# First batch of an attention and mixing kernel: more places for queries, later weight loads, a wider first mixing product, and another order of the opening

## The chip, the cores and the metric

The kernel runs on one core of one Trainium2 chip. The metric is the device time of one execution in microseconds (us). Engines are named as the profile names them: PE is TensorE, PEld its weight loads, DVE VectorE, ACT ScalarE, POOL GpSimd, SP SyncE; SPq is SP's issuing of DMAs.

## The reference

Attention over 4 batches, 8 heads, 768 tokens of width 64: each token sees a band of 16 neighbours on either side and 24 block summaries (maximum of the keys, mean of the values of each 32 tokens). Its output goes through a token mixing of rank 32 and a two-layer channel network of width 2048. Weights `U`, `V`, `w_ch1`, `w_ch2` come as 64-bit floats, all results are float32.

```python
k_sum = k.reshape(B, H, nb, block, D).max(axis=3)
v_sum = v.reshape(B, H, nb, block, D).mean(axis=3)
scores_all = np.concatenate([scores_l_masked, scores_s + np.log(block)], axis=-1)
a = softmax(scores_all)                          # 120 keys per 64 queries after packing
x = (a @ np.concatenate([v, v_sum])).reshape(B, S, 512)
u = x + (x.transpose(0, 2, 1) @ U @ V).transpose(0, 2, 1)
out = u + np.maximum(u @ w_ch1, 0.0) @ w_ch2
```

## The kernel before

Batches are done one after the other, each overlapping the next. Batch 0 has nothing to hide behind: its attention and mixing run in an opening of some 51 us, whose order is written by hand as a string of words, `START`. A loop takes the words one by one and records each word's instructions on the engines concerned; every engine then runs its own instructions strictly in that order, and SP issues the loads in that order. After the opening comes batch 0's channel network, 16 stretches `f`, each with a piece of up product and down product, with batch 1's attention spread between them.

The words, `h` a head, `i = 2h + a` a half of it:

- `lk h`, `lq h`, `lv p`, `lm`, `li`, `lu`, `lr`, `la f`, `lb f`: loads of keys, queries (two DMAs of 96 KB), values of two heads (two DMAs), mask, identity, `U` and `V` as raw 64-bit words, the matrix `rep`, one weight tile of `w_ch1` (`la`) or `w_ch2` (`lb`), 512 KB each.
- `K h`: two maxima over the keys on DVE (L316). `Kd h` / `Kp h`: their four copies into the key tile (L333), on DVE or POOL.
- `S h`: 12 score products on PE (L374). `E i`: three DVE instructions with the mask and the row maximum (L400, each with a read of its sum) and three exponentials on ACT (L410). `T i`: three transposes on PE (L460), `C i` their copy on ACT (L466). `V i`: six products with the values on PE (L476). `N h`: the division by the sum on DVE (L502 to L504), which writes `x`.
- `M g`: block means of the values of four heads on PE (L292), `Mo g` their copy on ACT (L304); `Bp`, `Dp`, `Bd`, `Dd`, `Ba` `h`: their 24-row copies into the value tiles (L337), on POOL (p), DVE (d) or ACT (a). `F` prepares the matrix for `M` on DVE.
- `X`, `Xt0` to `Xt2`, `Xs`, `Xl`: `U` and `V` from 64-bit words to float32 (ACT, POOL, DVE, DVE) and their split.
- `Z k`: scaling of weight step `k`'s raw words on ACT (L142); step 0 is tile (0,0), step k is tiles (0,k) and (1,k-1). `Y k.0`, `Y k.1`, `Y k.2`: the three steps from raw words to float32 (signs L155 on POOL or L157 on DVE, then L161 and L164 on DVE). `W k`: the split in a rounded high part (ACT, L179) and a low part (L180).
- `I c`, `Io c`, `J c`, `Jo c`: mixing's first and second product and their copies for channels c, c+1; `Q`, `Qo`: spreading of `V`. `G hf.c`, `Go hf.c`: three transposes and one product on PE (L699, L707) that make the mixed rows, and their split on ACT and DVE (L719, L720). `U 0.0`: the first up product (L927), which ends the opening.

Buffers that matter here: weight tiles have five places in a ring for each of the two matrices, `weight_place(i, f)`, reused with `f % 5`. While the ring is empty, other data are put there: `raw_uv`, the target of `lu`, is `weight_place(0, 2)`, the place of the tile that `la2` loads. Queries of batch 0 have four places, `qd0`, so that `lq4` to `lq7` wait on SP until `S0` to `S3` have read theirs. PSUM's eight banks go round. In the channel network, `traffic(f, i)` loads the tiles that come later.

## Time and profile before

| | |
|---|---|
| time, median of 3 runs (lowest to highest) | 648.07 us (647.09 to 650.53) |
| profiled execution: time, and its span | 648.17 us, 646.4 us |
| PE busy of the span | 627.1 us (97%) |
| DVE, ACT, POOL busy | 361.7, 354.6, 363.3 us |
| DMA | 115.39 MB, mean 179 GB/s |

Busy times are of the span; the time that runs give is 1.8 us above the span, for what lies outside the first and last instruction. "PE acc L949 x8" is eight matmul records that write tile `acc` from line 949; a float32 product with float32 operands makes two records, so `S` shows as 24, `V` as 12, `T` as 3, `M` as 96.

### The profile page before, as it was taken

The page shows a single profiled execution, that of the slowest core. Times are in us where ns is not written, and L with a number is a line of the kernel's source. Part 1 is how long each engine was busy: PE and PEld are TensorE (multiplying, and loading weights), DVE is VectorE, ACT ScalarE, POOL GpSimd, SP SyncE. Part 2 cuts the span into 40 slices and gives each one's busy share as a digit, 9 for nine tenths or more (in the row PEclk, how much of TensorE's full clock was granted, in tenths as well). Part 3 has the DMA queues.
Part 4 walks back from the last instruction along what each step waited for, and adds up shares of the span by engine and source line. Part 5 has one row for each costly group of instructions (what it writes and reads, how often), then busy time and mean ns, then how long its engine had stood idle before and what let it go on. Part 6 is the DMA issues. An engine that isn't in the chain of part 4 may idle for free.

```text
span 646.4 us, 14559 instructions
## 1 busy us (share of the span) xinstructions
PE 627.1 (97%) x5528; PEld 563.4 (87%) x5528; DVE 361.7 (56%) x1002; ACT 354.6 (55%) x788; POOL 363.3 (56%) x391
## 2 busy tenths in 40 slices
PE   5879999999999999999999999999999999999997
PEld 4669988888888899998888899998888899998886
DVE  5779767675857596566444645565544522242223
ACT  4756766656663657675453457775453455553321
POOL 3525977965766875862246765771344565653320
PEclk9999999999999999999999999999999999999999
DMA  9897588866675169896628367887431164342002
GB/s 236 223 380 222 160 296 267 229 201 189 214 232 176 46 213 290 243 265 174 180 78 218 113 204 222 258 258 203 144 116 58 60 183 142 115 131 66 32 1 99
DMA packets 68678, 115.39 MB, mean 179 GB/s; under 512 B 6912, under 2 KB 43648, under 8 KB 68608
## 3 DMA queue, kind: packets, MB, share of 16 engines
q1 hardware_dynamic: 68608, 114.45, 58.9%
q8 instruction: 44, 0.72, 0.5%
q14 instruction: 26, 0.21, 0.1%
HBM read 90.31 MB, written 24.12 MB: 177 GB/s over the span
## 4 chain that ended last, share of the span: by engine, by line
PE 87%; DMA 4%; DVE 3%; SPq 2%; ACT 2%; issue 1%; DVEq 0%; ACTq 0%
PE acc L1316 30%; PE ps_h L1215 27%; PE acc L949 10%; PE ps_h L927 9%; PE ps_x L490 3%; PE ps_s L374 2%; PE ps_s L351 2%; DMA place<-in_w 1%; PE ps_t L460 1%; SPq L215 1%; DMA kt<-in_k 1%; PE ps_u L699 1%; DMA place<-in_v 1%; DMA place<-in_q 1%; PE ps_m L665 1%
## 5 line engine op out<-in xcount | busy, mean ns | idle before, releaser
L180 POOL TENSOR_TENSOR parts<-whole,parts 128x512 fp32r<-128x512 f32 (+1 forms) x144 | 182.3, 1273 | 162.9 <-ACT parts L179 153.1
L1316 PE MATMUL acc<-gh,parts 128*128 128x256 f32 (+1 forms) x768 | 198.2, 340 | 0.0
L1215 PE MATMUL ps_h<-op,parts 128*128 128x384 f32 x1008 | 181.7, 337 | 0.1
L1215 PEld LDWEIGHTS ps_h<-op,parts 128*128 128x128 f32 x1008 | 174.3, 188 | 2.7 <-issue 1.1
L1316 PEld LDWEIGHTS acc<-gh,parts 128*128 128x128 f32 x768 | 132.9, 189 | 17.4 <-issue 1.7
L1316 PE MATMUL acc<-gl,parts 128*128 128x256 f32 (+1 forms) x384 | 129.8, 338 | 0.2
L1288 DVE SCALAR_TENSOR_TENSOR gl<-place,gh 128x768 fp32r<-128x768 f32 x48 | 55.3, 1151 | 71.3 <-ACT gh L1284 71.2
L179 ACT CAST parts<-whole 128x512 fp32r<-128x512 f32 (+1 forms) x144 | 83.3, 583 | 3.3 <-DMA whole<-up 1.0
L1316 PEld LDWEIGHTS acc<-gl,parts 128*128 128x128 f32 x384 | 72.8, 189 | 7.5 <-DVE gl L1288 0.8
L410 ACT ACTIVATE e<-e,neg 128x120 f32<-128x120 f32 x144 | 46.5, 386 | 51.4 <-DVE neg L400 46.9
L927 PE MATMUL ps_h<-place 128*128 128x384 f32 x384 | 74.3, 342 | 0.0
L1284 ACT ACTIVATE gh<-place 128x768 fp32r<-128x768 f32 x48 | 40.5, 844 | 57.1 <-PE acc L1316 48.5
L927 PEld LDWEIGHTS ps_h<-place 128*128 128x128 f32 x384 | 66.2, 188 | 1.4 <-issue 0.4
L949 PE MATMUL acc<-place,gh 128*128 128x512 f32 x192 | 67.3, 405 | 0.0
L155 POOL TENSOR_SCALAR val<-place 128x512 f32<-128x512 f32 (+1 forms) x30 | 47.7, 1607 | 25.9 <-ACT place L142 21.4
L180 POOL TENSOR_TENSOR place<-val,place 128x512 fp32r<-128x512 f32 x29 | 38.7, 1357 | 18.3 <-ACT place L179 18.3
L742 POOL TENSOR_TENSOR op<-tmp,op 128x384 fp32r<-128x384 f32 x24 | 26.3, 1108 | 32.9 <-ACT op L738 30.2
L949 PEld LDWEIGHTS acc<-place,gh 128*128 128x128 f32 x192 | 35.9, 188 | 7.6 <-POOL place L180 0.6
L400 DVE CUSTOM_DVE_ANT_0 e<-ps_s,mask_sb 128x120 f32<-128x120 f32 x144 | 32.8, 277 | 11.3 <-PE ps_s L351 5.9
L949 PE MATMUL acc<-place,gl 128*128 128x512 f32 x96 | 37.7, 393 | 0.1
L161 DVE SCALAR_TENSOR_TENSOR val<-place,val 128x512 int32<-128x512 int32 (+1 forms) x33 | 31.7, 965 | 3.3 <-POOL val L155 3.2
L1241 DVE TENSOR_TENSOR place<-place,ps_h 128x384 f32<-128x384 f32 x24 | 13.2, 551 | 36.2 <-PE ps_h L1215 36.2
(113 smaller groups left out, 796.5 us busy)
## 6 DMA issues: line engine op xcount, KB each, us to landing
place<-in_w SPq DMA_DIRECT2D x32, 512.0 KB, 5.6
whole<-up SPq DMA_DIRECT2D x24, 512.0 KB, 4.4
whole<-down SPq DMA_DIRECT2D x24, 512.0 KB, 4.3
whole<-up SPq DMA_DIRECT2D x24, 384.0 KB, 3.4
vt<-in_v SPq DMA_DIRECT2D x48, 146.2 KB, 3.8
kt<-in_k SPq DMA_DIRECT2D x24, 288.0 KB, 5.9
there<-squares SPq DMA_DIRECT2D x16, 384.0 KB, 4.3
at<-there SPq DMA_DIRECT2D x64, 96.0 KB, 3.5
```

The lines of the kernel that those rows point to most:

```text
L155: nc.gpsimd.tensor_scalar(f32(bits), f32(hi), 0.0, None, ALU.mult)
L161: lambda lo, hi, bits: nc.vector.scalar_tensor_tensor(bits, lo, 29, bits, ALU.logical_shift_right, ALU.bitwise_or),
L179: nc.scalar.copy(hi, val)
L180: engine.tensor_tensor(lo, val, f32(hi), ALU.subtract)
L400: nc.vector.tensor_tensor_reduce(out=e[:, u, :], in0=ps[:, i * KC : (i + 1) * KC], in1=mask_sb[:, m, :], scale=-SCALE, scalar=BIG, op0=ALU ...
L410: nc.scalar.activation(e[:, u, :], e[:, u, :], AF.Exp, bias=st.neg[h][:, u : u + 1], scale=-1.0,)
L927: nc.tensor.matmul(ps[:, :NH], w_split[0, f][:, c % 2, part_w, c // 2], ut[:, c, :], start=(n == 0), stop=(n == 3 * NC - 1),)
L949: nc.tensor.matmul(acc[t], gt[:, sl], w_split[1, f][:, part_w], start=(first and j == 0), stop=(last and j == 2),)
L1215: nc.tensor.matmul(ps, a[:, sa, i], b[:, sb, i], start=(first and n == 0), stop=(n == 5), skip_group_check=not first,)
L1284: nc.scalar.activation(gh, h, AF.Relu)
L1288: nc.vector.scalar_tensor_tensor(gl, h, 0.0, f32(gh), ALU.max, ALU.subtract)
L1316: nc.tensor.matmul(place, w[:, part_w, c * P : (c + 1) * P], gt[:, q0:q1], start=(f == 0 and i == 0 and j == 0), stop=(f == NF - 1 and j = ...
```

## The change

Four things, all in batch 0's opening. Queries get eight places: three in a spare tile and five in the weight places (1,2), (1,4) and (0,4). Weight tiles (0,4), (1,3) and (1,4) are no longer loaded in the opening but by `traffic` in the first stretches; their words are gone from `START`, and the loads that follow in the opening are `la0`, `la2`, `la1`, `lb0`, `lb2`, `lb1`, `la3`. Mixing's first product for two channels is six matmuls of 256 columns instead of twelve of 128. And all words stand in another order, in which step 1's signs (`Y1.0`) are made on POOL instead of DVE, and step 0's low part (`Wp0`) too.

```diff
 START = """
-    lm lk0 lq0 lk3 lu li lq3 X K0 Kd0 S0 K3 Kd3 E1 lk2 Xt0 lk1 S3 E0 K2 lq2 E7 Kp2 lq1 S2 E6 T6 E4
...
+    lk0 lk1 lq0 lm lq1 K0 Kd0 K1 Kd1 lk3 S0 lq3 S1 lk2 E0 E3 K3 E1 K2 lv0 E2 lq2 Kp3 S3 li lv1 E6
...
-    qd0 = [t[:, j * NH : (j + 1) * NH] for j in range(3)] + [weight_place(1, 2)[:, :NH]]
+    spare = [weight_place(1, 2), weight_place(1, 4), weight_place(0, 4)]
+    qd0 = [t[:, j * NH : (j + 1) * NH] for j in range(3)]
+    qd0 += [spare[i][:, j * NH : (j + 1) * NH] for i, j in ((0, 0), (1, 0), (1, 1), (2, 0), (0, 1))]
...
-        st.qt[h] = qd0[h % 4] if st.b == 0 else qz[h % 2].rearrange("p u q -> p (u q)")[:, :NH]
+        st.qt[h] = qd0[h] if st.b == 0 else qz[h % 2].rearrange("p u q -> p (u q)")[:, :NH]
...
+    def mix_t_wide(st, c):
+
+        ps = bank("ps_m")
+        for s in range(NU):
+            g = s % 4
+            nc.tensor.matmul(
+                ps[R * g : R * g + R, : 2 * P],
+                u_sb[:, s, :],
+                st.x[:, s, c * P : (c + 2) * P],
+                start=(s < 4),
+                stop=(s + 4 >= NU),
+                tile_position=(0, R * g),
+            )
+        st.ps_m[c] = ps
...
-            split(hi, lo, val, nc.vector if k < 2 else nc.gpsimd)
+            split(hi, lo, val, engine)
...
-    turns = {k: turn_weights(k) for k in range(2)}
+    turns = {k: turn_weights(k, k in (1,)) for k in range(2)}
...
-        "I": lambda c: mix_t(st, c, 2),
+        "I": lambda c: mix_t_wide(st, c),
...
-        "W": split_weights,
+        "W": lambda k: split_weights(k, nc.vector),
+        "Wp": split_weights,
...
-            if 0 < f and f + RING - 1 < NF:
+            if f + RING - 1 < NF:
                 load_weight(0, f + RING - 1)
...
-            if 1 < f and f + RING - 2 < NF:
+            if f + RING - 2 < NF:
                 load_weight(1, f + RING - 2)
```

The opening on PE, before and then after: `place` stands for the key and query tiles, `ps_s` for a bank of scores, `ps_t` for one of transposes, `ps_n` for the block means.

```order
L374 MATMUL ps_s<-place 64x120 x36
L460 MATMUL ps_t<-ident_sb,gl 120x128 x3
L460 MATMUL ps_t<-ident_sb,gh 120x128 x9
L374 MATMUL ps_s<-place 64x120 x12
L460 MATMUL ps_t<-ident_sb,gh 120x128 x3
L292 MATMUL ps_n<-place,means_w 32x65 x48
```

```order
L376 MATMUL ps_s<-place 64x120 x48
L462 MATMUL ps_t<-ident_sb,gl 120x128 x9
L462 MATMUL ps_t<-ident_sb,gh 120x128 x6
L294 MATMUL ps_n<-place,means_w 32x65 x48
L462 MATMUL ps_t<-ident_sb,gh 120x128 x6
L462 MATMUL ps_t<-ident_sb,gl 120x128 x3
```

Four heads' scores now stand ahead of the first transpose, where there were three.

The loads on SP around the first weight tiles, before and then after. `place` with `in_v` is a pair's values, with `in_w` a weight tile; in square brackets stand the semaphores that SP waits for ahead of the issue, `DMAHW` those of earlier DMAs and the others those of engines.

```order
L236 DMA place<-in_v 96x780 [waits DMAHW1_49]
L236 DMA place<-in_v 96x780 [waits DMAHW2_49]
L792 DMA place<-in_w 128x1024 [waits DMAHW3_49]
L792 DMA place<-in_w 128x1024 [waits DMAHW4_49]
L792 DMA place<-in_w 128x1024 [waits DMAHW5_49]
L1049 DMA rep_sb<-in_rep 128x128 [waits DMAHW6_49]
```

```order
L238 DMA place<-in_v 96x780 [waits DMAHW1_49]
L238 DMA place<-in_v 96x780 [waits DMAHW2_49]
L809 DMA place<-in_w 128x1024 [waits DMAHW3_49]
L809 DMA place<-in_w 128x1024 [waits DMAHW4_49,DMAHW6_49,DVE_49,Pool_49]
L1066 DMA rep_sb<-in_rep 128x128 [waits DMAHW5_49]
L809 DMA place<-in_w 128x1024
```

The second weight tile is now `la2`, which waits for the readers of `raw_uv` on POOL and DVE; it was the last one. Behind it on SP now stand `lr`, `lb0`, `la1` and the rest.

ACT at the end of the mixing, before and then after: `L142` / `L144` scales a weight tile (`Z1`), `t_st` is what `Jo` writes, `vm_st` what `Qo` writes, `t_862` and `t_855` what `Io` writes.

```order
L142 ACTIVATE place<-place 128x512 [waits DMAHW5_49]
L142 ACTIVATE place<-place 128x512 [waits DMAHW7_49]
L691 CAST t_st<-ps_r 128x256 [waits PE_49]
L1039 CAST vm_st<-ps_v 128x384 [waits PE_49]
L678 COPY t_862<-ps_m 128x256 [waits PE_49]
```

```order
L144 ACTIVATE place<-place 128x512 [waits DMAHW7_49]
L144 ACTIVATE place<-place 128x512 [waits DMAHW6_49]
L708 CAST t_st<-ps_r 128x256 [waits PE_49]
L181 CAST place<-val 128x2x256 [waits DVE_49]
L1056 CAST vm_st<-ps_v 128x384 [waits PE_49]
L695 COPY t_855<-ps_m 128x256 [waits PE_49]
```

`Z1` stands ahead of the same copies as before, and step 0's split has moved in between.

## The prediction

> **What bounds the kernel now.** I read the two windows on either side of the first up product first. Columns: length, then busy time and records of PE, PEld, DVE, ACT and POOL, granted clock, DMA share, GB/s.

> ```profile
> 0.00:51.10 51.10, 37.06 (x741) 30.43 (x742) 35.07 (x173) 30.51 (x86) 19.05 (x47) 1.00 0.95 281
> 51.10:646.40 595.30, 590.00 (x4789) 533.02 (x4788) 326.68 (x831) 324.12 (x703) 344.24 (x344) 1.00 0.56 170
> ```

> After 51.1 us PE is busy 590.0 of 595.3 us, and the change takes nothing from it there. In the opening PE is idle 14.0 us, with no other engine full and the DMA engines at 95%. So the change is worth what it does to the start of the first up product, 51.10; I look for that time alone. The timeline of PE gives pace and waits (start, length, what, idle before and its releaser):

> ```profile
> 5.37 1.99 PE L374 MATMUL ps_s<-place 64*64 64x120 f32 x24 [5.37 <-DVE place L333]
> ...
> 13.48 0.89 PE L460 MATMUL ps_t<-ident_sb,gl 128*120 128x128 f32 x3
> 14.17 2.13 PE L460 MATMUL ps_t<-ident_sb,gh 128*120 128x128 f32 x9
> ...
> 17.72 1.60 PE L292 MATMUL ps_n<-place,means_w 96*32 96x65 f32 x96
> ...
> 22.89 0.85 PE L374 MATMUL ps_s<-place 64*64 64x120 f32 x24
> ...
> 26.29 0.45 PE L476 MATMUL ps_x<-place 120*64 120x65 f32 x8 [0.54 <-issue]
> ...
> 35.20 1.19 PE L292 MATMUL ps_n<-place,means_w 120*32 120x65 f32 x68 [1.23 <-issue]
> ...
> 41.40 2.44 PE L476 MATMUL ps_x<-place 120*64 120x65 f32 x76 [2.10 <-issue]
> ...
> 48.06 0.49 PE L699 MATMUL ps_u<-ident_sb,x 128*128 128x128 f32 x3
> ...
> 48.56 0.49 PE L699 MATMUL ps_u<-ident_sb,x 128*128 128x128 f32 x3
> ...
> 51.10 4.51 PE L927 MATMUL ps_h<-place 128*128 128x384 f32 x24
> ```

> Two things stand in it. The same 24 score records take 1.99 us early and 0.85 later, three transposes 0.69 us early (13.48 to 14.17): PE starts at half pace, though the granted clock is 1.00. And three waits end by "issue", in the midst of equal matmuls, where no semaphore is due. Counted in the trace's PE records, these places are 256 instructions apart (a matmul record and its weight load are two). One DMA of the instruction queue falls before each:

> ```profile
> q8 instruction: 44, 0.72, 0.5%
> ```

> 0.72 MB in 44 is 16 KB, 256 instructions of 64 bytes. So PE gets its program in blocks of 256, and a block seems to be asked for when the one before is begun: 26.29 to 35.20 is 8.9 us, 35.20 to 41.40 is 6.2, both with the DMA engines full. PE's matmuls of such a block take 3 to 5 us in the opening, 22 later, so only the opening can wait for it.

> [...]

> Now SP and the loads: the longest of SP's waits (total, times, longest), its first weight tiles, and windows as above.

> ```profile
> SPq L215 <- PE ps_s L374: 4.6, 1, 4.6
> ```

> ```profile
> 27.55 1.38 SPq L792 DMA_DIRECT2D place<-in_w x3
> ```

> ```profile
> 2.20:18.00 15.80, 10.38 (x131) 7.98 (x135) 9.58 (x64) 7.23 (x23) 4.81 (x12) 1.00 1.02 269
> ...
> 18.00:20.00 2.00, 2.00 (x99) 1.91 (x88) 1.72 (x10) 2.00 (x9) 0.72 (x3) 1.00 0.62 178
> 20.00:22.00 2.00, 1.29 (x29) 0.97 (x26) 1.87 (x7) 2.00 (x7) 1.78 (x5) 1.00 0.45 109
> ...
> 36.00:40.00 4.00, 3.30 (x87) 2.80 (x76) 3.09 (x5) 3.48 (x10) 2.91 (x5) 1.00 1.03 404
> 60.00:70.00 10.00, 10.00 (x59) 9.18 (x58) 8.50 (x25) 6.88 (x20) 8.59 (x12) 1.00 0.33 113
> ```

> SP waits 4.6 us for a query place; 18 to 22 us the DMA engines are half empty for it. Weight tiles are issued from 27.55 on and come at 404 GB/s.

> **The change part by part.** *Eight query places* take that wait away. Up to the last values the loads are 7.0 MB, and at the 269 GB/s of the window to 18 us, in which SP did not hold them up, they land by 29 us, about 4 us sooner. What that is worth depends on who is late next, and that is the engines in the new order. Rows of the timelines for their steps:

> ```profile
> 4.22 0.61 DVE L316 TENSOR_REDUCE km<-place 128x6 f32<-128x192 f32 x2 [4.22 <-DMA place<-in_k]
> ...
> 4.87 0.79 DVE L333 COPY place<-km 64x48 f32<-64x48 f32 x4
> ...
> 8.34 0.28 DVE L400 CUSTOM_DVE_ANT_0 gh<-ps_s,mask_sb 128x120 f32<-128x120 f32 x1
> ...
> 9.36 0.28 DVE L400 CUSTOM_DVE_ANT_0 gh<-ps_s,mask_sb 128x120 f32<-128x120 f32 x1
> ...
> 15.37 0.56 DVE L161 SCALAR_TENSOR_TENSOR val<-place,val 128x384 int32<-128x384 int32 x1
> ...
> 19.86 0.36 DVE L337 COPY place<-vsum 24x390 f32<-24x390 f32 x1 [0.28 <-ACT vsum L304]
> ...
> 41.77 0.17 DVE L502 TENSOR_SCALAR sum<-ps_x 128x6 f32<-128x6 f32 x1 [1.56 <-PE ps_x L476]
> ...
> 42.67 0.15 DVE L502 TENSOR_SCALAR sum<-ps_x 128x6 f32<-128x6 f32 x1
> ...
> 48.49 0.43 DVE L693 TENSOR_TENSOR t_st<-ps_r,t_st 64x256 fp32r<-64x256 f32 x1
> ...
> 51.55 1.28 DVE L164 SCALAR_TENSOR_TENSOR val<-place,val 128x512 int32<-128x512 int32 x2
> ...
> 56.85 1.13 DVE L161 SCALAR_TENSOR_TENSOR val<-place,val 128x512 int32<-128x512 int32 x1 [0.17 <-POOL val L155]
> ...
> 10.71 1.04 POOL L333 COPY place<-km 64x48 f32<-64x48 f32 x4 [0.58 <-DVE km L316]
> ...
> 36.87 4.28 POOL L337 COPY place<-vsum 24x390 f32<-24x390 f32 x6 [6.09 <-ACT vsum L304]
> ...
> 55.16 6.37 POOL L155 TENSOR_SCALAR val<-place 128x512 f32<-128x512 f32 x4 [14.01 <-ACT place L142]
> ...
> 20.23 2.00 ACT L466 COPY place<-ps_t 120x384 f32<-120x384 f32 x5
> ...
> 40.42 1.34 ACT L142 ACTIVATE place<-place 128x512 f32<-128x512 f32 x2
> ```

> *The order, up to M0.* `lk0` is now first, so K0 begins 0.4 us sooner, at 3.8. S0 runs 5.2 to 7.2 (2.0 each at the early pace), S1, whose queries are 1.2 MB down the line, 7.5 to 9.5. A half E is 0.65 (8.34 to 9.36 is five steps). E3 needs S1, K3 stands behind E3 on DVE, Kp3 behind K3 on POOL, and S3 needs Kp3: 9.6 + 0.65 + 0.6 + half of 1.04 gives 11.5, S3 to 13.6. E6, then Kd2 (0.65, half of 0.79), then S2: 14.8 to 16.8. Five transposes at 0.69 make 20.3, some of them faster; M0 1.6 at full pace, so M0 ends at 21.6. Before it ended at 19.3: 2.3 us later.

> *From M0 to `la2`.* Mo0 at 21.8 frees DVE, which then has no gap: four vsum copies, three K, six E, to E9: 4 x 0.4 + 3 x 0.6 + 6 x 0.65 = 7.3, so 29.1. PE gets to V5 at 27.3: S6, V3, S5, V7, V0 run as their copies come, S4 follows Kp4 at 26.0, V2 after it (0.85 a score, 0.39 a V: 12 of the 76 records at 41.40). Counted through the new order (S 48 instructions, V 24, T 6, M 192, a wide product 24, and the semaphore instructions), the block borders now stand at S6's first matmul, in V5, in M1, at V8's first matmul and in the last G. S6 begins at 22.6 (it needs the bank that C3 frees, two ACT copies of 0.4 after Mo0). At that time the last values and `la0` are queued, as at 26.29 before. The block with V5 then takes between 6.2 and 8.9 us; I take the middle, 7.6: V5 waits until 30.2, 2.9 us. V1 follows, N0 can begin at 31.1 in place of 29.2 or so. N0, N1, N2 (0.9 each), E15, E14, N3, Xt1, Xt2 (0.56 each) make 6.0: Xt2 ends at 37.1.

> *`la2` behind Xt2.* That is where the change has a new wait. `la2` overwrites `raw_uv`, so SP stands from some 22 us until 37.1, and behind it `lr`, `lb0`, `la1`, all needed for J0 and Z1. From then three tiles and `rep` are 1.64 MB, 4.1 us at 404 GB/s; to this I add 2.0 for the way of a lone DMA (the mask's 2.6, the shortest in these rows of the DMA issues, less 0.6 for its bytes):

> ```profile
> mask_sb<-in_mask SPq DMA_DIRECT2D x1, 240.0 KB, 2.6
> place<-in_w SPq DMA_DIRECT2D x10, 512.0 KB, 9.2
> ```

> So `la1` lands at 43.2. By the row of `in_w`, with eight DMAs in flight, it would be 46.3; 6.1 is nearer to what an empty queue gives.

> *Z1 to the first up product.* The path: first half of Z1 0.67 (43.9), signs on POOL twice 1.59 (47.1), L161 of the second tile 0.9 (0.64 alone, 1.13 beside POOL; 48.0), two L164 1.4 (1.28 alone; 49.4), Jo2's subtraction behind them on DVE 0.43 (49.8). G0.2's product then runs, and three more G at 0.5 (48.06 to 48.56): 51.65. Before it was 51.10: 0.55 us later. The signs on POOL cost 3.2 on this path, where DVE did both in 0.76. Beside this path lie M1, its seven POOL copies (0.71 each), V8 to V15 and N7, which end at about 44, and Io2 at 46.

> *Step 0's low part on POOL* (1.36) ends by 48.5, needed in the last third of U 0.0, at 53; its cover is 4 us. *The wide product*: 12 records of 256 columns for 24 of 128; between 0.5 less per product (the records' number) and 0.2 more; I take 0, since Jo2 waits for DVE and not for I2. *Three weight tiles later* (`la4`, `lb3`, `lb4`): 1.5 MB less in the opening and the same more between 52 and 62, where the share falls to 0.33; they are due a stretch of some 9 us after issue: nothing. If that cover were gone, 3.9 us of DMA would stand before Z4.

> Sum: 0.55 us on the profiled execution's 648.17, which is 0.1 above the median of 648.07: 648.6.

> **Rivals.** *The block comes in time* (no wait in V5): N0 at 29.2, the rest 1.9 us sooner, 49.75, so 646.7. For it: the wait at 26.29 was only 0.54. Against: then the DMA engines had been half empty before. [...]

> *The opening runs at full pace after S1.* S3 0.9, S2 0.9, five T at 0.33: M0 ends 3 us sooner. With the block in time too, 46.7, so 643.7, faster by more than 0.5%; with the block late again, 7.6 after an S6 at 19.6, N0 comes at 28.1 and the end is 645.6. For it: S0 and S1 are now back to back. Against: in the trace 1.9 us of scores and 2.7 of transposes, 4.6 in a row, ran at the slow pace. [...]

> *The tiles behind `la2` land late* (the other side). Decided on SP: if the DMA for `la1` takes the 9.2 us of the `in_w` row and not 6.1, the end is 3.1 later, 651.7; with the longest block (8.9) 653.0. From 2.7 us over the 51.65 on, it is slower by more than 0.5%.

> *The query places bring nothing*: SP no longer waits, but la0 aside nothing needed is earlier. This is part of the forecast.

> **How the numbers follow.** 0.5% is 3.2 us, about what a measurement of this kernel can tell from none. Forecast, a block late at V5 and `la2` behind Xt2, 648.6: 0.45. Block in time, 646.7: 0.17. Full pace early and block in time, 643.7: 0.17. Tiles late, 651.7 to 653: 0.21. So faster 0.17, same 0.62, slower 0.21. The range leaves out the ends of the two last: 645.0 to 651.8. Forecast's own range by its block, 6.2 to 8.9: 647.2 to 649.9.

> **What would show it.** SP's issue of `la2` in the changed trace, right after Xt2 on DVE, at 35 to 38, with the DMA share near zero before; ACT's Z1 waiting for `in_w` until 41 to 45; an "issue" wait of PE of 1.5 to 4 us among the V of head 2; M0 ending at 21 to 22; no "issue" wait in V8. Wrong would be: Xt2 before 33.5, Z1 without wait, or first up product before 48 or after 54.

## The result, and the profile after

| | before | after |
|---|---|---|
| time, median of 9 runs each (lowest to highest) | 648.46 us (647.00 to 650.53) | 656.61 us (651.90 to 659.00) |
| profiled execution: time, span | 648.17, 646.4 us | 655.95, 654.2 us |
| start of the first up product | 51.10 us | 59.51 us |

The changed kernel takes 1.011 times the time of before (95% interval 1.0076 to 1.0144): slower by 7 us by this ratio, by 8 us by the medians, and above the forecast range. The same two windows of the changed kernel, with the columns explained in the prediction:

```profile
0.00:51.10 51.10, 35.57 (x685) 27.92 (x685) 30.35 (x163) 27.23 (x78) 18.69 (x46) 0.97 0.76 207
51.10:654.20 603.10, 595.48 (x4819) 538.88 (x4819) 330.43 (x837) 327.65 (x712) 346.34 (x347) 1.00 0.57 174
```

The DMA share of the first 51.1 us fell from 0.95 to 0.76, and the granted clock is below 1. From the first up product to the end it is 594.7 us (654.20 less 59.51), where it was 595.3: the loss is all in the opening. PE's timeline there:

```profile
16.32 1.89 PE L376 MATMUL ps_s<-place 64*64 64x120 f32 x24 [2.55 <-DMA place<-in_q]
...
21.53 1.94 PE L294 MATMUL ps_n<-place,means_w 96*32 96x65 f32 x96
...
25.24 0.96 PE L376 MATMUL ps_s<-place 64*64 64x120 f32 x24 [0.64 <-issue]
...
32.02 1.02 PE L478 MATMUL ps_x<-place 120*64 120x65 f32 x22 [1.95 <-issue]
...
33.80 1.57 PE L478 MATMUL ps_x<-place 120*64 120x65 f32 x24
35.30 1.15 PE L376 MATMUL ps_s<-place 64*64 64x120 f32 x24
...
56.28 0.55 PE L724 MATMUL ps_u<-vm_st,t_st 128*128 128x384 f32 x1 [2.10 <-DVE t_st L710]
...
59.51 4.50 PE L944 MATMUL ps_h<-place 128*128 128x384 f32 x24
```

The waits that end by "issue" stand at the borders that the prediction counted, at S6 (where it priced no wait) and within V5. And behind two waits of some 2 us the work runs slowly: 24 records of V take 1.57 us, where 24 such had taken 0.92 at 27.41. Two windows show why; the eighth number is the granted clock, the ninth the DMA share:

```profile
33.00:36.40 3.40, 3.40 (x53) 2.78 (x52) 2.56 (x9) 0.00 (x0) 0.00 (x0) 0.56 0.11 34
...
56.50:60.00 3.50, 3.50 (x15) 3.30 (x15) 3.00 (x7) 2.45 (x6) 0.00 (x0) 0.52 1.08 323
```

TensorE was granted about half its clock for one stretch after each wait (0.56 and 0.52 in these windows). In the profiled execution of before, the opening has no such stretch once its first products are past: the granted clock is 1.00 from 16.17 us, its first clock record, to 51.10. The first window also has the DMA engines almost idle, because SP stands:

```profile
26.61 14.81 SPq L809 DMA_DIRECT2D place<-in_w  x2
41.47 0.43 SPq L1066 DMA_DIRECT2D rep_sb<-in_rep  x1
41.94 2.38 SPq L809 DMA_DIRECT2D place<-in_w  x5
```

`la0` and `la2` are one group, 14.8 us long: `la2` is held until Xt2 has read the projections, and `lr`, `lb0`, `la1` stand behind it. The chain from there on, one row each of DVE (Xt2), ACT (Z1), POOL (the signs) and DVE again (the last L163, and Jo2's subtraction):

```profile
40.45 0.56 DVE L166 SCALAR_TENSOR_TENSOR val<-place,val 128x384 int32<-128x384 int32 x1
...
48.94 1.22 ACT L144 ACTIVATE place<-place 128x512 f32<-128x512 f32 x2 [4.08 <-DMA place<-in_w]
...
49.77 3.00 POOL L157 TENSOR_SCALAR val<-place 128x512 f32<-128x512 f32 x2 [4.21 <-ACT place L144]
...
52.80 1.76 DVE L163 SCALAR_TENSOR_TENSOR val<-place,val 128x512 int32<-128x512 int32 x1 [0.37 <-POOL val L157]
...
55.80 0.43 DVE L710 TENSOR_TENSOR t_st<-ps_r,t_st 64x256 fp32r<-64x256 f32 x1
```

### The profile page after: what moved, and what is told of

Read it like the earlier page. It is cut to its first block, busy times and chain, and to the rows that moved or that the text cites. A ratio compares the mean times of both kernels' runs of the same rounds, so it can differ in the third digit from the quotient of the medians.

```text
span 654.2 us, 14512 instructions
## 1 busy us (share of the span) xinstructions
PE 631.0 (96%) x5504; PEld 566.8 (87%) x5504; DVE 360.8 (55%) x1000; ACT 354.9 (54%) x789; POOL 365.0 (56%) x392
## 4 chain that ended last, share of the span: by engine, by line
PE 89%; DMA 3%; DVE 2%; ACT 2%; issue 1%; SPq 1%; POOL 1%; POOLq 0%; DVEq 0%; ACTq 0%
PE acc L1334 30%; PE ps_h L1233 27%; PE acc L966 10%; PE ps_h L944 9%; PE ps_x L492 3%; PE ps_s L376 3%; PE ps_t L462 2%; PE ps_s L353 2%; PE ps_u L716 1%; DMA place<-in_q 1%; DMA place<-in_w 1%; PE ps_u L724 1%; PE ps_m L682 1%; PE ps_x L478 1%; SPq L217 1%
## 5 line engine op out<-in xcount | busy, mean ns | idle before, releaser
L1302 ACT ACTIVATE gh<-place 128x768 fp32r<-128x768 f32 x48 | 40.5, 844 | 57.1 <-PE acc L1334 48.5
L157 POOL TENSOR_SCALAR val<-place 128x512 f32<-128x512 f32 (+1 forms) x32 | 50.4, 1591 | 27.2 <-ACT place L144 16.9
L759 POOL TENSOR_TENSOR op<-tmp,op 128x384 fp32r<-128x384 f32 x24 | 26.3, 1106 | 32.9 <-ACT op L755 30.2
L402 DVE CUSTOM_DVE_ANT_0 e<-ps_s,mask_sb 128x120 f32<-128x120 f32 x144 | 32.7, 276 | 11.5 <-PE ps_s L353 6.0
L163 DVE SCALAR_TENSOR_TENSOR val<-place,val 128x512 int32<-128x512 int32 (+1 forms) x33 | 32.9, 998 | 4.6 <-POOL val L157 4.5
L957 DVE SCALAR_TENSOR_TENSOR gl<-ps_h,gh 128x384 fp32r<-128x384 f32 x32 | 17.7, 554 | 29.6 <-ACT gh L956 29.4
## 6 DMA issues: line engine op xcount, KB each, us to landing
place<-in_w SPq DMA_DIRECT2D x32, 512.0 KB, 5.7
whole<-up SPq DMA_DIRECT2D x24, 512.0 KB, 3.9
whole<-down SPq DMA_DIRECT2D x24, 512.0 KB, 4.1
```

What stands on the lines that cost most here:

```text
L157: nc.gpsimd.tensor_scalar(f32(bits), f32(hi), 0.0, None, ALU.mult)
L163: lambda lo, hi, bits: nc.vector.scalar_tensor_tensor(bits, lo, 29, bits, ALU.logical_shift_right, ALU.bitwise_or),
L402: nc.vector.tensor_tensor_reduce(out=e[:, u, :], in0=ps[:, i * KC : (i + 1) * KC], in1=mask_sb[:, m, :], scale=-SCALE, scalar=BIG, op0=ALU ...
L1302: nc.scalar.activation(gh, h, AF.Relu)
```

## The experiments

Two readings were possible. A: `la2` and what stands behind it make the kernel late. B: the order itself does, through TensorE's waits for its program (called D below) or through its clock (C). Ratios are to runs of before on the same chip, with 95% intervals; "first up" is the start of the first up product in the profiled execution. The changed kernel has 1.011 and 59.51.

### Without the hold, and three parts alone

`a_uv13`, the changed kernel with `raw_uv` in a place that nothing loads into early:

```diff
-    raw_uv = weight_place(0, 2, I32)[:, : 4 * NU * R]
+    raw_uv = weight_place(1, 3, I32)[:, : 4 * NU * R]
```

> The changed kernel, with the raw U and V put into weight place (1,3) in place of (0,2), so that the load la2 has nothing to wait for; all else, the order too, as changed. Theory A (the tiles behind la2 are what is late: la2 is held 14.8 us, Z1 waits 4.1 us for in_w): SP issues la2 near 27 us, Z1 no longer waits, the first up product comes 4 to 6 us sooner, 650.5 to 652.5. Theory B (the opening's order and PE's program blocks are what is late): Z1 moves up, but PE is no sooner ready; with the DMA engines full from 27 to 40 us the issue waits of PE in M1 and V8 come back with 1 to 2 us each, and the time falls by less than 2 us, 654.5 or more.

650.45 us, ratio 1.0034 (1.0010 to 1.0058), first up 53.33. Without the hold most of the loss is gone: A. About 2 us stay, and the trace shows TensorE's waits, with slow stretches around two of 1.86 and 2.35 us early on and behind the one shown (PE's timeline, then windows with the clock eighth):

```profile
24.68 0.96 PE L376 MATMUL ps_s<-place 64*64 64x120 f32 x24 [2.30 <-POOL place L339]
```

```profile
13.00:20.20 7.20, 5.54 (x76) 4.88 (x80) 4.25 (x32) 4.33 (x14) 1.15 (x6) 0.56 1.09 249
26.50:29.90 3.40, 3.40 (x72) 2.91 (x64) 2.70 (x21) 3.05 (x11) 2.42 (x7) 0.56 1.03 213
```

Three parts were put alone into the kernel before. `b_q8`: only the eight query places.

> The kernel before with eight query places alone. Theory A: SP's wait of 4.6 us goes, the last values land some 3 us sooner, M1 with them: 645 to 647. Theory B: the same loads then keep the DMA engines full at 17 to 22 us, PE's blocks come later and PE's order is the same: within 1 us of before, 647.5 to 649.5.

649.42 us, ratio 1.0014 (1.0001 to 1.0027), first up 52.42. No gain from the places. The loads come sooner (SP has issued the last values at 25.7 us for 27.5 before), and the first up product does not.

`b_late`: only the three weight tiles loaded in the first stretches.

> The kernel before with three weight tiles (la4, lb3, lb4) loaded in the first stretches alone. Both theories: 1.5 MB less in the opening, nothing waits for these tiles; under theory B the block at V (issue wait 2.1 us at 41.4) may come 0.5 to 1 us sooner. 647.5 to 648.5; over 650 would mean that the tiles are late in the stretches.

649.12 us, ratio 1.0001 (0.9984 to 1.0019). No change, as costed. In its profiled execution, the second longest of twelve (650.77 us), the first up product came at 53.87: such a start can be 2 us and more off in one execution, and small differences in it say little.

`b_wide`: only the wide first product.

> The kernel before with mixing's first product 256 columns wide alone. Theory A: no effect, 648 to 648.6. Theory B: 48 instructions fewer in PE's program move the last block borders of the opening by one or two products; the wait at 47.8 goes and the first up product comes 0.3 to 1 us sooner, 647.3 to 648.

647.48 us, ratio 0.9983 (0.9965 to 1.0001), first up 50.96. The second wide product takes 1.06 us, in `b_late`, with 24 narrow records, 1.03, so on TensorE it is worth nothing, as costed; the 0.0017 of the ratio are not clear of noise.

### The hold, by the order alone

`c_la2`, the changed kernel with the projections where they were:

```diff
-    E14 Xt0 N3 T9 Xt1 Xt2 la2 lr M1 Z0 T14 Mo1 T15 Y0.0 lb0 Bp6 Xs Dp6 C13 Dp5 C11 I0 C9 Y0.1 Bp5
-    V12 V13 Xl Ba4 C8 Y0.2 V11 C14 N6 la1 Dp4 Io0 Dp7 C15 V10 V8 V9 V15 Bp7 V14 N5 Z1 N4 Y1.0 J0 N7
+    E14 Xt0 N3 T9 Xt1 Xt2 lr M1 Z0 T14 Mo1 T15 Y0.0 lb0 Bp6 Xs Dp6 C13 Dp5 C11 I0 C9 Y0.1 Bp5
+    V12 V13 Xl Ba4 C8 Y0.2 V11 C14 N6 la1 la2 Dp4 Io0 Dp7 C15 V10 V8 V9 V15 Bp7 V14 N5 Z1 N4 Y1.0 J0 N7
```

> The changed kernel with one word of its order moved: the third up tile (la2) is asked for behind la1 instead of ahead of lr, lb0 and la1; the projections stay in weight place (0,2). Theory A (what stood behind la2 in SP's queue made the changed kernel late, not the place and not la2's own landing): la0 is issued without a wait behind it, la1 lands before the DVE is at the signs, the first up product starts at about 53.3 us as with the projections in place (1,3), and the time is 650.5 (649.5 to 651.5), ratio to before 1.003. Theory B (order of the opening and PE's program alone): 655 to 657, first up product at 58 to 60. If la2's own landing beside lr, lb0 and la1 costs something, 651 to 653.

650.29 us, ratio 1.0041 (1.0019 to 1.0063), first up 53.26. The place is as in the changed kernel, only what stands behind `la2` differs: what costs is the queue behind the wait. ACT's Z1, with no wait for `in_w` ahead of it:

```profile
43.95 1.28 ACT L144 ACTIVATE place<-place 128x512 f32<-128x512 f32 x2
```

### The clock

`c_warm`: `a_uv13` with three products of 128x384 whose result is written over, in TensorE's waits ahead of S3 and S2:

```diff
         ps = [bank("ps_s") for _ in range(2)]
+        for _ in range({3: 1, 2: 2}.get(h, 0) if st.b == 0 else 0):
+            nc.tensor.matmul(
+                ps[0][:, :NH], st.qt[1][:, :P], st.qt[1][:, :NH], start=True, stop=True
+            )
```

> The changed kernel with the projections in place (1,3), and three more TensorE products (128x384 f32, written over afterwards, 12 instructions in all): one ahead of S3 and two ahead of S2, where TensorE waited 1.86 and 2.35 us. Theory C (the half clock from 12.9 to 19.7 us sets the time: TensorE is busy there from 14.7 us on): S2, the five transposes and M0 at full clock, M0 ends 2.5 us earlier, at 18.7, and the first up product starts at 51 instead of 53.3; time 648.2, and more runs at a granted clock of 1.0. Theory D (TensorE waits for the next 256 instructions of its program, asked for when S2 ends and 8.4 us on the way, whatever the clock): M0 ends earlier, but S6 starts at 23.9 for 24.7, first up product 52.6, time 649.8. No effect of either: 650.5.

648.33 us, ratio 0.9996 (0.9977 to 1.0015), first up 52.10. By the time it is C: the rest of `a_uv13`'s loss is gone. The first up product, at 52.10, lies between the two readings (51 and 52.6), and the trace shows D beside C: M0 ends at 19.4, and TensorE then waits for its program:

```profile
14.53 1.30 PE L380 MATMUL ps_s<-place 64*64 64x120 f32 x24
...
23.49 0.68 PE L466 MATMUL ps_t<-ident_sb,gh 128*120 128x128 f32 x2 [3.49 <-issue]
```

`e_warm02`: the same three products in the changed kernel itself, `la2`'s hold left in.

> The changed kernel as it is (projections in place (0,2), la2 ahead of lr, lb0 and la1) with the three wide warming products of the kernel with place (1,3) ahead of S3 and S2. It tells whether the two causes add. Adding (the projections are given free by a chain that runs through TensorE and then ACT and POOL, so 2.2 us of half clock come off that too): 656.6 less 2.1 makes 654.5 (653.3 to 655.3), ratio to before 1.009, first up product at 57.4. Not adding (with la2 held, the loads and the block of 256 instructions at V5 set when the projections are freed, and what TensorE gains ahead of them is waited away): 656 to 657, ratio 1.011 or more, first up product at 59 or later.

650.52 us, ratio 1.0050 (1.0026 to 1.0074), first up 52.81: by the ratios 3.9 us less than the changed kernel, where 2.1 were expected by adding; the two intervals do not meet. S2 now runs at full pace, no wait for the program is left at V5, and SP is free 6.2 us sooner (35.23 for 41.42). From there to the first up product it is 17.6 us, in the changed kernel 18.1. The slow stretch behind V5 is gone too, and with it the chain on DVE from N0 to Xt2 takes 6.04 us (28.78 to 34.82), where it took 7.93 in the changed kernel (33.08 to 41.01):

```profile
16.64 0.85 PE L380 MATMUL ps_s<-place 64*64 64x120 f32 x24
```

```profile
28.78 0.16 DVE L508 TENSOR_SCALAR sum<-ps_x 128x6 f32<-128x6 f32 x1
...
34.26 0.56 DVE L166 SCALAR_TENSOR_TENSOR val<-place,val 128x384 int32<-128x384 int32 x1
```

```profile
26.42 8.81 SPq L813 DMA_DIRECT2D place<-in_w  x2
```

So the two causes are one chain: what delays the readers of `raw_uv` delays `la2`, `la1` and the first up product by about as much. In the five traces with the hold it is 17.2 to 19.2 us from SP's release to the first up product, for releases from 35.2 to 41.8.

`f_tiny02`: the same three products with 32 columns for 384, so the same instructions in the program, but little to fill the waits with.

> The changed kernel with three products ahead of S3 and S2 as in the warmed one, but 32 columns wide for 384: the same 12 instructions, the same borders in TensorE's program, and only some 0.4 us each for waits of about 2 us. Theory C (the clock: filling the waits is what took 4 us off): S3 to M0 at half clock as in the changed kernel, ratio 1.010 to 1.012, 655 to 657. Theory D (the borders, 12 instructions earlier, one of them off S6 and one within V): 650.5 to 652, ratio 1.005, as with the wide ones. In between, 652.5 to 654.5, if both count.

654.29 us (median of 6), ratio 1.0087 (1.0069 to 1.0105), first up 57.13: in between. In this profile the early work ran at half clock, that behind V5 did not (a last stretch, from 54.5, did again):

```profile
13.70:20.50 6.80, 5.31 (x50) 4.61 (x54) 3.96 (x30) 3.94 (x13) 1.19 (x5) 0.51 1.08 257
30.00:36.40 6.40, 6.40 (x189) 5.49 (x188) 5.40 (x32) 4.38 (x15) 2.12 (x5) 1.00 0.40 112
```

Of the fall from 1.011 to 1.0050, 0.0023 come with the narrow products, which is not clear of noise, and 0.0037 more with the wide ones. For that second step the two intervals give a noise of some 0.003, so it is just clear of it: the same 12 instructions bring more when they fill the waits. The borders alone, which would have given 1.005, do not explain the wide products' gain; whether they bring a part of it is not settled. The projections are free sooner in both (SP at 37.96 and 35.23).

`c_warmg`: the changed kernel with two products of 128x384 ahead of G0.2, in the wait for `t_st`.

> The changed kernel with two more TensorE products (128x384 f32, written over afterwards, 0.78 us each at full clock) ahead of the transposes of G0.2, where TensorE waited 2.10 us for the copy of the mixed rows. Theory C (the wait of about 2 us lets the granted clock fall to half for the next 3.4 us, and so the last five products of the mixing took 0.96 us each for 0.51): no half-clock stretch at 56 to 60 us, the last products at 0.5 us each, first up product at 58.0 (57.7 to 58.3) instead of 59.5, time 655.1. Rival (the copies of the results to ACT and DVE, or the program's blocks, set that pitch): pitch 0.9 or more as before, first up product at 59.5 to 60.2, time 656.6 to 657.3.

654.51 us (median of 4), ratio 1.0111 (1.0068 to 1.0153): the time shows no gain. The mechanism is in the trace all the same. The slow stretch came earlier, behind the 1.77 us wait for `vm_st`, and the last G stand 0.51 us apart (54.89 to 55.40) for 0.96. (Its first up product came at 56.92, but SP had been free 1.7 us sooner as well, which these products cannot have done.)

```profile
50.70:54.10 3.40, 3.40 (x14) 2.94 (x13) 3.00 (x5) 1.19 (x3) 1.59 (x2) 0.51 1.10 298
54.10:57.00 2.90, 2.90 (x20) 2.41 (x20) 2.30 (x5) 1.37 (x4) 0.00 (x0) 1.00 1.04 328
```

### TensorE's program

`c_twelve`: `a_uv13` with thirteen products of 128x32 ahead of S3 (52 instructions).

> The changed kernel with the projections in place (1,3), and thirteen small TensorE products (128x32 f32, 52 instructions, written over afterwards) ahead of S3. They move the borders of TensorE's blocks of 256 instructions 52 forward: one falls at the end of S3 instead of the end of S2, the next into M0 instead of at S6. Theory D (blocks): the block for S6 is asked for at about 12.3 us instead of 16.4, comes at about 20.7, and the 2.30 us wait ahead of S6 is gone or under 0.4 us; S6 starts at 22 to 22.5 for 24.7, first up product at 51 (50.5 to 51.8), time 648.3. Theory C alone (clock; the small products may keep it up or not): S6 still starts at 24 or later, with a wait of over 1.5 us ahead of it, first up product 52.6 or later, time 649.8 or more. If the DMA queues are as full at 12 as at 16 us the block may take longer than 8.4 us; S6 would then start between the two.

650.73 us, ratio 1.0035 (1.0010 to 1.0061), first up 55.46. The small products took 5.75 us, more than the 1.86 us wait that they stood in, and S3 began at 15.79 for 10.94; so the times expected say nothing. But the wait ahead of S6 is gone, and the next stands 52 instructions earlier in the work, within a head's scores:

```profile
26.16 0.85 PE L380 MATMUL ps_s<-place 64*64 64x120 f32 x24
...
30.72 0.62 PE L380 MATMUL ps_s<-place 64*64 64x120 f32 x11 [0.41 <-issue]
```

`d_start`: `c_warm` with eleven such products ahead of S0, from 0.98 us on.

> The kernel with the projections in place (1,3) and three wide warming products, and eleven small products more (128x32 f32 of zeros, 44 instructions) ahead of S0, from 0.95 us on, where TensorE had nothing to do until 5.8. Theory D (blocks): the border that stood ahead of the last transposes falls 44 instructions earlier in the program's work, into M0, and the one before it to the end of S3 instead of the end of S2; its block is asked for at about 12.9 for 15.9 us and is there at 20.5 (7.6 us as with the three products alone), where TensorE waited until 23.5. S6 starts at 22 for 24.7, first up product at 50.4 (49.8 to 51.2) for 52.1, time 646.8, below before. Theory C as well: S0 and S1 at full clock (1.0 us each for 2.0), which frees DVE and ACT earlier. Rival (after the clock is up, the loads of queries, keys and values set the opening, not the program): a wait for DMA or for POOL takes the place of the 3.49 us, first up product 51.8 to 52.5, time 648.3.

649.36 us, ratio 1.0016 (0.9997 to 1.0034), first up 52.34: by that start the rival, by the trace neither. The second border moved into M0, where D had it, and waits 1.39 us for 3.49 (S0 still took 2.05 us, against C). No wait for DMA or POOL took its place, as the rival had it, but two later borders now wait longer:

```profile
21.29 0.48 PE L294 MATMUL ps_n<-place,means_w 96*32 96x65 f32 x17 [1.39 <-issue]
...
34.95 1.97 PE L294 MATMUL ps_n<-place,means_w 96*32 96x65 f32 x88 [2.04 <-issue]
...
48.47 0.48 PE L704 MATMUL ps_r<-t,rep_sb 128*128 128x256 f32 x1 [1.09 <-issue]
```

Waits for the program add to 5.0 us here and 5.5 in `c_warm`: here moving a border moved the wait.

`d_wstart`: `b_wide` with the same eleven products.

> The kernel before with the wide first product, and the same eleven small products ahead of its first scores. Before has no half-clock stretch once it is warm, at 16 us, and only 0.54 us of wait at its second border. Theory C (the clock at the start counts): scores and transposes up to 16 us at full clock, 1 to 2 us of TensorE time less, first up product at 50.0 to 50.5 for 50.96, time 646.8. Rival (there the keys' loads and the DVE set the pace up to 33 us): 647.5, first up product at 50.8 to 51.3; or slower, 648 to 649, if a border falls where it stops more.

646.81 us, ratio 0.9989 (0.9969 to 1.0010): not told apart from `b_wide`.

### The signs, and a version that beats both

`f_signs`: the changed kernel with `Y1.0` on DVE (`turn_weights(k)` for both steps).

> The changed kernel with the signs of the second stretch's two tiles on the DVE as before (0.42 us each there for 1.50 us each on POOL). The tail theory (la1's chain Z1, signs, shifts, Jo2 sets the first up product): the signs no longer wait for POOL, and the shift in L163 that ran beside POOL takes 0.88 for 1.76 us; Jo2 ends 2.0 us earlier, first up product at 57.5 for 59.5, time 654.6, ratio 1.008. Rival (TensorE's own work or the copies of the results set it): 656 to 657, ratio 1.011.

655.03 us (median of 12), 1.011 times before's median, as the changed kernel; the ratio without its three longest runs is 1.0086 (1.0059 to 1.0113). First up 60.17. The expected 2 us are not to be seen. DVE, with its rows in order:

```profile
50.10 0.99 DVE L159 TENSOR_SCALAR val<-place 128x512 int32<-128x512 int32 x2 [3.04 <-ACT place L144]
51.01 0.16 DVE L504 TENSOR_SCALAR sum<-ps_x 128x6 f32<-128x6 f32 x1
...
52.47 1.48 DVE L163 SCALAR_TENSOR_TENSOR val<-place,val 128x512 int32<-128x512 int32 x2
...
56.49 0.43 DVE L710 TENSOR_TENSOR t_st<-ps_r,t_st 64x256 fp32r<-64x256 f32 x1 [1.34 <-ACT t_st L708]
```

The signs are quick there (0.99 us for both, 3.00 on POOL), but they wait 3.04 us for Z1 with N7 queued behind them, and N7 is what I2, J2 and Jo2 need. With `la1` this late, the signs on POOL are not shown to cost anything.

`e_both`: the kernel before with the later weight tiles and the wide product.

> The kernel before with two parts of the change alone: the three weight tiles loaded a stretch later, and the wide first product. From the two single runs (ratios 1.0001 and 0.9983): if they add, 0.998, 647.2; from the first up product on the changed kernel took 0.7 us less than before (594.7 for 595.4), so if that comes with the later loads and the opening is as in the wide kernel (50.96), the span is 645.6 and the time 647.3, or 0.997 and 646.6 at best. Rival (the later loads shift where the program's blocks and the half clock fall in the opening, first up product at 52 to 54 as in the run with the later loads alone): 648.5 to 649.5, ratio 1.000 to 1.001.

646.62 us, ratio 0.9968 (0.9948 to 0.9989): the one version here whose interval lies below before, by 0.3%; it was not run a second time. First up was at 51.83, no earlier than before, in a profiled execution that was the slowest of its twelve (649.05 us); so where its gain comes from is open.

## Why the prediction was wrong

Much of the mechanism was right: the opening decides, the query places bring nothing, TensorE waits for its program at V5, `la2` behind Xt2 is the new wait, and the path through Z1, signs, shifts and Jo2 sets the end. What it lacked is a clock that falls again after a wait. The forecast 0.55 us was 8.41. Of the prediction's marks, the wait at V5, the empty DMA engines and the V8 without a wait came as said; M0, `la2`'s issue, Z1 and the first up product all came later than the bounds given for them. Its terms:

| step | forecast | trace | late by |
|---|---|---|---|
| M0 ends | 21.6 | 23.5 | 1.9 |
| S6 begins | 22.6 | 25.2 | 2.6 |
| V5 goes on | 30.2 | 32.0 | 1.8 |
| Xt2 ends | 37.1 | 41.0 | 3.9 |
| `la1` landed (Z1 begins) | 43.2 | 48.9 | 5.7 |
| first up product | 51.65 | 59.51 | 7.9 |

- **The step that failed** is the pace of TensorE in the opening. I took the half pace as a matter of the start, over by M0, and read "granted clock 1.00" in before as given; that column shows 1.00 also ahead of a trace's first clock record (16.17 us in before), where the same 24 score records took 1.99 us for 0.85. In the changed kernel half pace comes back after a wait. The wait at V5 brought a half-clock stretch (0.50 from 32.57 to 35.98), and N0 to Xt2, put at 6.0 us, took 7.9. In the four traces with such a stretch at that place (this one, `c_warmg`, `f_signs`, `c_la2`) it is 7.4 to 8.1, in the six with the same words and no stretch there 6.0 to 6.6. The wait for `t_st` brought a second stretch (0.50 from 56.46 to 59.87), and the last three G and their pitch took 2.9 us for 1.5. I had looked at the clock only as a way to be faster.
- **The lateness of M0** belongs to this one execution. `lq2` landed late, so S2 came 1.5 us late, and the early half pace lasted into M0. In four other traces with the same words up to there M0 ended at 21.1 to 22.0, as forecast (`c_la2`, `c_warmg`):

```profile
19.50 1.59 PE L294 MATMUL ps_n<-place,means_w 96*32 96x65 f32 x96
...
20.04 1.59 PE L294 MATMUL ps_n<-place,means_w 96*32 96x65 f32 x96
```

- **The wait at S6** was put at nothing, though the prediction had counted a border there. In these five traces TensorE stood 0.64 to 2.30 us ahead of S6, and S6 began at 23.3 to 25.2 for 22.6.
- **`la1`'s landing** was mis-sized: 7.5 us from SP's release, where I took 6.1 from bytes and a lone DMA. In `e_warm02` it is 7.4, in `f_tiny02` 8.8: between the forecast's figure and the 9.2 of the rival.
- **Z1 to the first up product** took 10.6 us for 8.45: the slow G, and the second L163, 1.76 us for 0.9. That one ran beside step 0's low part, which the change had moved to POOL and which the prediction took as covered; in `f_signs`, mostly clear of it, two such take 1.48. The signs themselves were right (3.0 for 3.2).

```profile
52.73 1.29 POOL L182 TENSOR_TENSOR place<-val,place 128x512 fp32r<-128x512 f32 x1
```

- **The wait at V5** was 1.95 us for 2.9, in the range given, and the border stood where it was counted. M1 and V8 had none. The prediction's 3 to 5 us for the matmuls of a block in the opening are 4.1 to 6.1 in before's trace (126 records from 41.40 to 47.50); no sum hung on it.
- **The rivals.** "The block comes in time" did not hold here, but did in `e_warm02`. "Tiles behind `la2` late" had the right place, and 651.7 to 653 was too little, since it left Xt2 at 37.1, or 38.4 with the longest block. "Opening at full pace" had the clock right and its sign wrong: the changed order, with its waits of 1.95 and 2.10 us, has two stretches of 3.41 us at 0.50 in the opening, before has none behind its first record at 16.17 us. Half pace for twice that length stands early in `f_tiny02`, 6.80 us at 0.51.

Not every such wait brings a slow stretch: the 2.10 us at 41.40 in before did not, nor `b_wide`'s 2.06, while 1.92 us in `e_both` did (0.62 over the 4.50 us from 37.00 on). The traces of before and of the changed kernel show a difference. The clock's records last 10.24, 3.41, 20.48, 3.41 and 593.92 us in the changed kernel from 22.33 to 653.79 (three, one, six, one and 174 times the shortest), and 631.47 us in before from 16.17 to past its end (185 times). Cut at such times, the stretches around the waits are these, the changed kernel first, then before (behind the bounds stand length and PE's busy time; the clock is eighth):

```profile
29.15:32.57 3.42, 1.47 (x46) 1.17 (x38) 2.41 (x22) 3.23 (x12) 1.88 (x6) 1.00 1.04 263
32.57:35.98 3.41, 3.41 (x54) 2.83 (x52) 2.56 (x9) 0.00 (x0) 0.00 (x0) 0.50 0.25 81
...
49.63:53.05 3.42, 1.69 (x11) 1.49 (x12) 1.80 (x3) 3.01 (x9) 3.28 (x3) 1.00 1.01 398
53.05:56.46 3.41, 1.31 (x11) 1.04 (x10) 3.35 (x5) 0.45 (x2) 0.96 (x1) 1.00 1.12 270
56.46:59.87 3.41, 3.41 (x15) 3.21 (x16) 2.90 (x7) 2.32 (x6) 0.00 (x0) 0.50 1.08 324
```

```profile
36.65:40.06 3.41, 2.65 (x50) 2.15 (x40) 3.15 (x5) 3.41 (x11) 2.97 (x5) 1.00 1.04 408
40.06:43.48 3.42, 2.08 (x71) 2.08 (x72) 1.72 (x7) 1.70 (x4) 1.03 (x2) 1.00 1.02 406
43.48:46.89 3.41, 3.41 (x60) 2.53 (x56) 3.21 (x11) 1.59 (x5) 0.00 (x0) 1.00 1.04 385
```

In the changed kernel 1.95 and 2.10 us of idle time in one such stretch were followed by half clock, 1.73 us were not. Before's 2.10 us fall on two, 0.76 us in one and 1.34 in the other, and were not. `f_tiny02` shows both: the 3.01 us ahead of 49.15 fall on two, 1.50 and 1.51, and escape, while the 2.10 us ahead of 54.08 lie within one:

```profile
44.23:47.64 3.41, 1.91 (x31) 0.98 (x23) 0.00 (x0) 0.89 (x2) 0.08 (x1) 1.00 1.00 382
47.64:51.05 3.41, 1.90 (x12) 1.68 (x13) 2.01 (x3) 3.00 (x9) 3.41 (x3) 1.00 1.07 363
51.05:54.47 3.42, 1.32 (x11) 1.05 (x10) 3.36 (x5) 0.25 (x1) 0.76 (x1) 1.00 1.07 329
54.47:57.88 3.41, 3.41 (x16) 3.26 (x15) 3.08 (x8) 2.72 (x7) 0.00 (x0) 0.50 1.11 303
```

This is read from three traces and was not put to an experiment. If it holds, the same wait costs more in one execution than in the next, by where these stretches begin.

## What to carry to other kernels

When a load is put into a place that still holds live data, look at what stands behind it in the queue, and forecast the last reader of that data with all its delays: here a late opening was passed on almost one for one. Price a new TensorE wait of 2 us as the wait and up to 1.7 us more for the half clock behind it (an estimate, half of the 3.41 us that the changed kernel's stretches last), and check whether the work there has slack. A few wide products, written over later, in such waits can be worth their trouble: three of them took 4 us off the changed kernel.
